# Retention scores without a repeated last chunk, weighed in four pieces instead of two

## The chip, the core and the metric

The kernel runs on one core of a Trainium2 chip. A core has a matrix engine (TensorE, PE in the profile), a vector engine (VectorE, DVE), an activation engine (ScalarE, ACT), a general engine (GpSimd, POOL) and a queue engine that issues the transfers (SyncE, SP). Each has its own list of instructions and runs it in order; they meet at semaphores. PE writes into PSUM, which has eight banks here, each 128 partitions by 512 float32 words. The metric is the device time of one execution in microseconds (us).

## The reference

Two blocks in a row, in float32. The first is retention with a decay per head, the second a gated feed-forward network on the result:

```
q, k, v: (8, 8, 576, 64)          batch, heads, positions, head size
scores = q @ k.T / sqrt(64)       per batch and head, 576 x 576
D[i, j] = gamma_head ** (i - j) if i >= j else 0
ret = scores * D
attn = ret @ v                    -> x of 4608 tokens x 512
xn = x / sqrt(mean(x * x) + 1e-6) * rms_g
out = (silu(xn @ w_gate) * (xn @ w_val)) @ w_out      512 -> 1536 -> 512
```

## The kernel before

**Retention in chunks.** The 576 positions of a head are cut into nine chunks of 64 (`NC` = 9, `L` = 64). Inside a chunk the kernel computes the 64x64 scores and weighs them (the decay and the causal triangle); what earlier chunks give to later ones goes through a 64x64 state per chunk, k transposed times v, that is carried on with a decay. Two heads make one job: with 8 batches and 4 pairs of heads there are 32 jobs, `j` = 0 to 31. `FIRST` is 8, so "the ninth job on" means `j` >= 8, 24 jobs.

**Where a product sits in the array.** Head `e` of the pair has its q and k in partitions `side(e)`, that is 0 to 63 or 64 to 127. All products of retention are 64x64, so each uses a quarter of the PE array: a half of its rows (where the operands lie) and a half of its columns (where the result goes in PSUM). A float32 product shows in the profile as two weight loads and two matmul records.

**The steps of a job:**

- `scores(j)` (product in line 295): for chunk `c` and head `e` the result goes to bank `s[e]`, partitions `side(c odd)`, columns 64 i on, with `i` = c // 2. Nine chunks leave the last column block (256 to 319) with its lower partitions alone, since there is no tenth chunk. The loop therefore runs to `NC + 1` = 10 and repeats chunk 8 for the upper partitions: 20 products for the two heads.
- `states(j)` (line 318): 16 products k.T v, into bank `s[2]`, into the free right part of `s[1]` and into bank `last`.
- `weigh(j)` (line 331): DVE multiplies the scores by a power of gamma and by the triangle and writes tile `ret`, 128 partitions by 5 x 64 for each head. One operation per head, 128x320. `ret` has one buffer.
- `sums(j)` (lines 362 and 344 for `j` >= 8): eight DVE operations that run along the chunks, each on the one before, and read the states out of PSUM.
- `values(j)` (line 382): 18 products of `ret` and v into two banks `av`. Odd chunks read partitions 64 to 127 of `ret`, even ones 0 to 63; for chunk 8, which is even, only partitions 0 to 63 of the last block are read, and v comes from the small tile `vt`.
- `carried(j)` (line 402): 16 products of `sum` and q that add onto `av`; ACT then copies `av` to x (line 426).

**The order.** `slot(j)` puts a job's work on the engines: values(j-1), scores(j), states(j), weigh(j), carried(j-1), sums(j). So a job's `ret` and `sum` are used one slot later. Jobs 0 to 11 are placed by a list of steps (`PLAN`) in the first 250 us, among the preparation of the weights and plain products (`up_plain`, line 762). The later jobs are placed by loops at the end: for each token block `u` from 2 on, six calls of `up(u, n)`, each with seven products of eight records (line 702, banks x, y, z, x, w, z, w), and a slot after some of them. After `up` comes `across` (line 872). DVE adds the products of `up` up (lines 709 and 721) and takes differences (line 786).

**Banks.** All PSUM tiles turn round one pool of eight banks. A slot takes six (two av, three s, one last), an `up` four (x, y, z, w). So the banks that `scores` fills are, one `up` later, the banks of the next products, and PE may write them only when DVE has read them. The framework finds these waits by itself from the regions that instructions read and write, and puts them on instructions; where one instruction has more waits than it can hold, a separate waiting instruction (EVENT_SEMAPHORE in the profile) is put in front.

Of the kernel before, what the change touches and what calls it, by code (L numbers as in the profile page):

```python
# [13 lines left out]
ALU = mybir.AluOpType  # L14
P = 128
L = P // 2
# [3 lines left out]
def _gamma(H):  # L20
    return 1.0 - 2.0 ** (-5.0 - np.arange(H, dtype=np.float64))
# [23 lines left out]
def kernel(  # L45
# [11 lines left out]
    nc = tc.nc  # L57
    B, H, S, D = q.shape
# [4 lines left out]
    NC = S // L  # L63
    NFULL = S // P
    TAIL = S - NFULL * P
# [7 lines left out]
    FIRST = 2 * NHP  # L73
# [15 lines left out]
    def bank(name):  # L89
        return banks.tile([P, 512], F32, tag="b", name=name)  # L90
# [23 lines left out]
    causal = const.tile([P, L], F32, name="causal")  # L114
# [167 lines left out]
    def side(i):  # L282
        return slice(i * L, i * L + L)
# [3 lines left out]
    def scores(j):  # L287

        d = st[j]
        s = d["s"] = [bank(f"s_{j}_{i}") for i in range(3)]  # L290
        for c in range(NC + 1):
            i, odd = divmod(c, 2)
            c = min(c, NC - 1)
            for e in range(2):
                nc.tensor.matmul(  # L295
                    s[e][side(odd), i * L : i * L + L], lhsT=d["kT"][side(e), c * L : c * L + L],
                    rhs=d["qT"][side(e), c * L : c * L + L], start=True, stop=True,
                )
# [24 lines left out]
    def weigh(j):  # L323

        d = st[j]
        hp = jobs[j][1]
        s = d["s"]
        n = NFULL + 1
        ret = d["ret"] = att.tile([P, 2, n, L], F32, tag="ret", name=f"ret_{j}", bufs=1)
        for e in range(2):  # L330
            nc.vector.scalar_tensor_tensor(
                out=ret[:, e], in0=s[e][:, : n * L].rearrange("p (c k) -> p c k", k=L),
                scalar=float(_gamma(H)[2 * hp + e] ** -L),
                in1=causal.unsqueeze(1).to_broadcast([P, n, L]), op0=ALU.mult, op1=ALU.mult,
            )

    def sums(j):

# [95 lines left out]
    def slot(j, rest=True):  # L434

        if rest:
            values(j - 1)
        scores(j)
        states(j)
        weigh(j)  # L440
        if j < FIRST:
            sums(j)
        if rest:
            carried(j - 1)
        if j >= FIRST:
            sums(j)
# [959 lines left out]
```

## Time and profile before

| | |
|---|---|
| time, median of 3 runs | 1101.61 us (1100.7 to 1102.21) |
| the profiled execution: its time, its span | 1100.22 us, 1098.4 us |
| granted TensorE clock, mean | 0.997 |
| ACT busy, POOL busy | 328.2 us (30%), 443.8 us (40%) |
| DMA, HBM | mean 222 GB/s; 211.92 MB read, 30.08 MB written |
| products of `up_plain`, line 762 | 384 records, 594 ns mean |
| products of `up`, line 702 | 2352 records, 379 to 382 ns mean by tile |

The page of a profile gives the busy time of each engine, its share of the span, the chain of work that ended last, and groups of instructions by line. The timeline lists instructions in order of time, with equal ones that follow each other merged: start, length, engine, line, operation, tiles, shape, count, and in brackets how long the engine had been idle before and what ended that. Matmuls overlap, so the merged length of a group is from its first start to its last end, and the distance from one start to the next says more than a length.

### The profile page before, as it was taken

The numbers are of one execution on the slowest core, as the hardware profiler recorded it, in microseconds if no ns is written. First come the engines' busy times: TensorE is split into PE (matmuls) and PEld (weight loads), VectorE is DVE, ScalarE is ACT, GpSimd is POOL, SyncE is SP. The second block draws the span as 40 slices with busy tenths as digits, with TensorE's granted clock in tenths as the row PEclk, the third lists the DMA queues.
The fourth block names the chain that finished last, engine by engine and source line by source line (L and its number), as shares of the span: only waits on it lengthen the run. The fifth ranks groups of instructions, "written<-read, shape, count | busy, mean of one in ns | idle before, by whom it ended". The sixth has DMA issues, their size and how long they took to land.

```text
span 1098.4 us, 24471 instructions
## 1 busy us (share of the span) xinstructions
PE 1085.5 (99%) x10102; PEld 912.2 (83%) x10102; DVE 727.2 (66%) x1251; ACT 328.2 (30%) x739; POOL 443.8 (40%) x421
## 2 busy tenths in 40 slices
PE   9899999999999999999999999999999999999998
PEld 7744444479988899889988998899888988998898
DVE  3878468877866774677667855677565735674467
ACT  5755564331124412332034203330233111201110
POOL 0026326538430195027702571237321932383236
PEclk9999999999999999999999999999999999999999
DMA  8756787596978876797678865888475755585471
GB/s 210 178 190 235 297 252 214 194 354 176 292 276 226 221 256 225 185 240 241 245 217 200 290 257 148 243 255 291 136 204 198 280 194 174 195 287 160 146 250 42
DMA packets 253871, 243.60 MB, mean 222 GB/s; under 512 B 193216, under 2 KB 213824, under 8 KB 247616
## 3 DMA queue, kind: packets, MB, share of 16 engines
q1 hardware_dynamic: 252320, 241.64, 69.7%
q8 instruction: 79, 1.29, 0.5%
q10 hardware_dynamic: 1440, 0.40, 0.2%
q14 instruction: 32, 0.26, 0.1%
HBM read 211.92 MB, written 30.08 MB: 220 GB/s over the span
## 4 chain that ended last, share of the span: by engine, by line
PE 97%; DVE 1%; issue 1%; ACT 0%; POOL 0%; POOLq 0%; DVEq 0%; ACTq 0%
PE up L762 15%; PE x L702 14%; PE w L702 13%; PE z L702 13%; PE y L702 7%; PE xo L872 6%; PE xp L872 4%; PE zo L872 4%; PE zp L872 3%; PE wo L872 2%; PE yo L872 2%; PE av L382 2%; PE av L402 2%; PE wp L872 2%; PE s L295 2%; PE yp L872 2%
## 5 line engine op out<-in xcount | busy, mean ns | idle before, releaser
L762 PE MATMUL up<-x,ring 128*128 128x512 f32 x384 | 167.1, 594 | 0.0
L702 PE MATMUL x<-x,ring 128*128 128x256 f32 x672 | 161.0, 382 | 0.0
L702 PE MATMUL w<-sums,ring 128*128 128x256 f32 x672 | 158.9, 379 | 0.0
L702 PE MATMUL z<-x,ring 128*128 128x256 f32 x672 | 158.7, 379 | 0.0
L824 POOL TENSOR_TENSOR vi<-h 128x384 f32<-128x384 f32 x32 | 42.4, 1326 | 275.9 <-DVE h L721 266.4
L762 PEld LDWEIGHTS up<-x,ring 128*128 128x128 f32 x384 | 72.2, 190 | 89.3 <-issue 84.7
L702 PEld LDWEIGHTS z<-x,ring 128*128 128x128 f32 x672 | 127.7, 190 | 17.4
L702 PEld LDWEIGHTS w<-sums,ring 128*128 128x128 f32 x672 | 127.6, 190 | 17.4
L702 PEld LDWEIGHTS x<-x,ring 128*128 128x128 f32 x672 | 125.3, 190 | 17.5 <-ACT m L728 0.2
L829 POOL TENSOR_TENSOR vi<-h 128x384 f32<-128x384 f32 (+2 forms) x46 | 43.9, 954 | 149.2 <-DVE h L721 149.2
L1068 POOL TENSOR_TENSOR vi<-vi 128x512 f32<-128x512 f32 (+1 forms) x77 | 78.2, 1028 | 51.9 <-DVE vi L899 35.5
L702 PE MATMUL y<-sums,ring 128*128 128x256 f32 x336 | 79.4, 379 | 0.0
L728 ACT COPY m<-x 128x512 f32<-128x512 f32 x42 | 24.6, 587 | 173.3 <-PE x L702 173.3
L709 DVE TENSOR_TENSOR h<-u,w 128x512 f32<-128x512 f32 x42 | 28.9, 688 | 67.8 <-PE w L702 67.8
L702 PEld LDWEIGHTS y<-sums,ring 128*128 128x128 f32 x336 | 63.8, 190 | 8.7
L709 DVE TENSOR_TENSOR u<-m,y 128x512 f32<-128x512 f32 x42 | 28.8, 686 | 63.2 <-PE y L702 62.5
L723 ACT ACTIVATE h<-h 128x512 f32<-128x512 f32 x63 | 39.7, 629 | 83.3 <-DVE h L709 83.3
L1188 POOL TENSOR_TENSOR vi<-vi 128x512 f32<-128x512 f32 (+1 forms) x24 | 40.7, 1696 | 30.4 <-DVE vi L1177 16.9
L709 DVE TENSOR_TENSOR u<-u,z 128x512 f32<-128x512 f32 x42 | 28.9, 687 | 33.6 <-PE z L702 33.4
L1188 POOL TENSOR_TENSOR ring<-ring 128x512 f32<-128x512 f32 x24 | 30.4, 1273 | 49.6 <-DMA w_up_blocks<-ring 43.9
L426 ACT COPY x<-av 128x192 f32<-128x192 f32 (+6 forms) x136 | 37.8, 278 | 30.0 <-PE av L402 28.5
L829 POOL TENSOR_TENSOR vi<-h,vi 128x384 f32<-128x384 f32 (+2 forms) x46 | 44.5, 968 | 3.6
(327 smaller groups left out, 2039.2 us busy)
## 6 DMA issues: line engine op xcount, KB each, us to landing
ring<-w_out_blocks SPq DMA_DIRECT2D x59, 1344.0 KB, 6.4
ring<-w_up_blocks SPq DMA_DIRECT2D x42, 1792.0 KB, 7.7
w_out_blocks<-vi SPq DMA_DIRECT2D x21, 448.0 KB, 6.2
out_dram<-vi SPq DMA_DIRECT2D x64, 128.0 KB, 3.1
qraw<-in_q_dram SPq DMA_DIRECT2D x96, 72.0 KB, 4.7
kraw<-in_k_dram SPq DMA_DIRECT2D x96, 72.0 KB, 2.7
k<-in_k_dram SPq DMA_DIRECT2D x48, 128.0 KB, 2.8
v<-in_v_dram SPq DMA_DIRECT2D x48, 128.0 KB, 3.1
```

Of the source, the lines that this page charges most:

```text
L295: nc.tensor.matmul(s[e][side(odd), i * L : i * L + L], lhsT=d["kT"][side(e), c * L : c * L + L], rhs=d["qT"][side(e), c * L : c * L + L], ...
L426: nc.scalar.copy(out=o, in_=part)
L702: nc.tensor.matmul(ps[:, i * HU : i * HU + HU], lhsT=w[:, PLACE[blk], c, i * P : i * P + P], rhs=t_of[u][blk][:, c], start=(start and i == ...
L709: nc.vector.tensor_tensor(out=o, in0=a, in1=pairs_of(ps), op=ALU.add)
L723: nc.scalar.activation(out=o, in_=c, func=AF.Silu)
L728: nc.scalar.copy(out=s1, in_=pairs_of(x_))
L762: nc.tensor.matmul(ps, lhsT=w[:, PLACE[blk], c % 2, i * P : i * P + P], rhs=x_of[u][:, c], start=(c == 0), stop=(c == NHP - 1),)
L824: eng.tensor_tensor(out=i1, in0=x12, in1=x11, op=ALU.subtract)
L829: eng.tensor_tensor(out=o[:, c], in0=a[:, c], in1=b[:, c], op=op)
L872: nc.tensor.matmul(ps, lhsT=lhs[:, c], rhs=w[:, s, c], start=((nm, s // 4) not in first), stop=False, skip_group_check=True,)
L1068: eng.tensor_tensor(out=t[:, :, o], in0=t[:, :, x], in1=t[:, :, y], op=ALU.add)
L1188: nc.gpsimd.tensor_tensor(out=t[o], in0=t[x], in1=t[y], op=op)
```

## The change

From the ninth job on, `scores` runs over the nine chunks alone: 18 products instead of 20. The upper partitions of the last block are then never written, so `weigh` may not read them: it weighs the four full blocks of each head in one operation (128 partitions by 256), and the last block in one more (64 partitions by 64). Jobs 0 to 7 keep the 20 products and the two operations.

```
-        for c in range(NC + 1):
+        for c in range(NC + (j < FIRST)):
...
-        for e in range(2):
-            nc.vector.scalar_tensor_tensor(
-                out=ret[:, e], in0=s[e][:, : n * L].rearrange("p (c k) -> p c k", k=L),
-                scalar=float(_gamma(H)[2 * hp + e] ** -L),
-                in1=causal.unsqueeze(1).to_broadcast([P, n, L]), op0=ALU.mult, op1=ALU.mult,
-            )
+        cuts = [(P, 0, n)] if j < FIRST else [(P, 0, NFULL), (TAIL, NFULL, n)]
+        for p, a, z in cuts:
+            for e in range(2):
+                nc.vector.scalar_tensor_tensor(
+                    out=ret[:p, e, a:z],
+                    in0=s[e][:p, a * L : z * L].rearrange("p (c k) -> p c k", k=L),
+                    scalar=float(_gamma(H)[2 * hp + e] ** -L),
+                    in1=causal[:p].unsqueeze(1).to_broadcast([p, z - a, L]),
+                    op0=ALU.mult, op1=ALU.mult,
+                )
```

Set side by side, the instruction lists of the two programs differ on two engines. On PE 48 products are gone, and there are 22 more separate waiting instructions: in the 20 calls of `up` that follow a slot, the first product into bank z now waits for DVE and for PE itself (an earlier product, some 40 products back), where before it waited for DVE alone; the other two stand in the part placed by the list. On DVE 48 operations 128x320 are replaced by 48 of 128x256 and 48 of 64x64. ACT, POOL and SP have the same instructions in the same order.

## The prediction

> **What bounds the kernel now.** I read the page first. PE is busy in 99% of the span, and the chain that ended last is PE.
>
> ```profile
> PE 1085.5 (99%) x10102; PEld 912.2 (83%) x10102; DVE 727.2 (66%) x1251; ACT 328.2 (30%) x739; POOL 443.8 (40%) x421
> ...
> PE 97%; DVE 1%; issue 1%; ACT 0%; POOL 0%; POOLq 0%; DVEq 0%; ACTq 0%
> ```
>
> So time can come only from work that PE no longer does, or go into a new wait of PE. A busy PE may still hide slack between records, so I read one slot in PE's timeline, job 21's (values of 20 first):
>
> ```profile
> 561.65 0.69 PE L382 MATMUL av<-ret,v 64*64 64x64 f32 x32
> 562.17 0.23 PE L382 MATMUL av<-ret,vt 64*64 64x64 f32 x2
> 562.19 0.27 PE L295 MATMUL s<-qT,kT 64*64 64x64 f32 x2
> 562.23 0.23 PE L382 MATMUL av<-ret,vt 64*64 64x64 f32 x2
> 562.28 0.70 PE L295 MATMUL s<-qT,kT 64*64 64x64 f32 x36
> 562.80 0.23 PE L318 MATMUL s<-v,k 64*64 64x64 f32 x1
> 562.81 0.22 PE L295 MATMUL s<-qT,kT 64*64 64x64 f32 x2
> ...
> 563.90 0.48 PE L702 MATMUL x<-x,ring 128*128 128x256 f32 x1
> ```
>
> From 562.28 to 562.80 lie 36 records of scores in 0.525 us. A record alone lasts 0.218, so several run at once: four at a time, one on each quarter of the array, is nine steps of 0.0583 us. A quarter does one record per step. The two products of the last value chunk (four records, `vt`) sit on two quarters only, and still the next full step of scores comes two steps later (562.17 to 562.28, 0.11 us): a half-filled pack costs what a full one does.
>
> Next, a slot with more waits in front of its states (job 22, keys and values arriving later):
>
> ```profile
> 576.18 0.69 PE L382 MATMUL av<-ret,v 64*64 64x64 f32 x32
> ...
> 576.81 0.75 PE L295 MATMUL s<-qT,kT 64*64 64x64 f32 x38
> 577.38 0.59 PE L318 MATMUL s<-v,k 64*64 64x64 f32 x26
> ...
> 578.46 0.48 PE L702 MATMUL x<-x,ring 128*128 128x256 f32 x1
> ```
>
> It takes 2.28 us to the next `up`, against 2.25: here the states start after the last score, not among them. Read in the same way, 13 slots have 2.28, six 2.25, and three more (jobs 9, 14, 30: 3.10, 3.64, 2.36). Job 14's holds a pause of PE of 1.06 us inside `carried`, with no releaser named.
>
> Then DVE behind the first of these slots:
>
> ```profile
> 564.42 0.88 DVE L331 SCALAR_TENSOR_TENSOR ret<-s,causal 128x320 f32<-128x320 f32 x2
> 565.22 0.21 DVE L362 COPY sum<-s 128x64 f32<-128x64 f32 x1
> 565.47 1.86 DVE L344 SCALAR_TENSOR_TENSOR sum<-sum,gc,s 128x64 f32<-128x64 f32 x6
> 567.44 0.28 DVE L344 SCALAR_TENSOR_TENSOR sum<-sum,gc,last 128x64 f32<-128x64 f32 x1
> 567.73 0.69 DVE L709 TENSOR_TENSOR u<-m,y 128x512 f32<-128x512 f32 x1
> 569.38 0.69 DVE L709 TENSOR_TENSOR u<-u,z 128x512 f32<-128x512 f32 x1 [0.97 <-PE z L702]
> ```
>
> DVE works through without a gap until 568.42, then waits 0.97 us for PE. And the one place where PE waits for this chain, jobs 8 and 9, where two slots are only one `up_plain` apart:
>
> ```profile
> 204.70 0.75 DVE L1177 SCALAR_TENSOR_TENSOR vi<-ring,exp 128x256 f32<-128x256 f32 x2
> 205.37 0.88 DVE L331 SCALAR_TENSOR_TENSOR ret<-s,causal 128x320 f32<-128x320 f32 x2
> 206.17 0.21 DVE L362 COPY sum<-s 128x64 f32<-128x64 f32 x1
> 206.42 1.86 DVE L344 SCALAR_TENSOR_TENSOR sum<-sum,gc,s 128x64 f32<-128x64 f32 x6
> 208.07 0.62 PE L318 MATMUL s<-v,k 64*64 64x64 f32 x26 [0.39 <-issue]
> ```
>
> The states of job 9 reuse a bank that the sums of job 8 read, and PE starts them 0.1 us after the fifth of the six sums ended.
>
> **The change, part by part.** *48 products fewer on PE.* Count the products of one slot by quarter, as rows half and columns half. Rows 0, columns 0: values 5 (even chunks, head 0), scores 5 (even chunks, head 0), states 4, carried 4: 18. Rows 0, columns 1: 5 + 5 + 4 + 4 = 18. Rows 1: 4 + 5 + 4 + 4 = 17 on each column half. Now the slot's time: 36 records at 0.0583 are 2.10 us, and 2.25 is this plus the fill and the drain before `up`. So the slot's time agrees with the need of its fullest quarter. The removed pair sits on columns 1, one product on each rows half. That leaves 18, 17, 17, 16: the fullest quarter is untouched, and its neighbour only idles for two steps, as in the `vt` pack. Gain by this count: 0. If PE went by the number of products in four-wide packs instead, a pack is gone, 2 x 0.0583 = 0.117 us, times 24 = 2.8 us. These are the ends; I take 0, because the `vt` pack is the nearest row and shows the half-filled price.
>
> *The gap before the states.* In the 13 slots of 2.28 us (and jobs 14 and 30, of the same kind) the states lose 0.036 us because PE has not passed their waits when the scores run out. With four records fewer to issue, PE's queue comes to these waits a step, 0.058, earlier, while the scores' fullest quarter ends when it did: the 0.036 should vanish, 14 x 0.036 = 0.5 us gained. Other end: the four records were cover, and the gap grows by their step, 24 x 0.058 = 1.4 us lost. I take -0.5, since the quarter that ends last does not move.
>
> *22 more waiting instructions on PE.* Queued behind each of the 20 in `up` are the z product and all of PE's later work. Its first term, PE itself, is some 40 products old; its second, DVE, is the weighing: ended at 565.30, needed by z at 567.46, so 2.16 us are left. 33 such instructions of line 702 exist already, each 51 ns on PE's queue, and products go on starting 1.72 or 1.73 us apart across them: PE's queue runs ahead of the array. Cost 0; the other end is in the rivals.
>
> *Weighing in four.* The trace has no 64x64 operation of this kind. Two 128x320 start 0.88 - 0.48 = 0.40 us apart, two 128x256 (line 1177) 0.75 - 0.417 = 0.333 apart. The 64 columns between them are 0.067, so the part that doesn't depend on size is 0.067 and 64 columns make 0.134. Four operations then take 2 x 0.333 + 2 x 0.134 = 0.93 instead of 0.80: +0.13 us per job. Upper end: the copy of 64 columns, after which the next started 0.25 us later: 2 x 0.333 + 2 x 0.25 = 1.17, +0.37. The new ones do not read each other as the copy's successor does, so I take +0.13: 3 us of DVE over 24 jobs.
>
> [...]
>
> What hides it: in `up`, the 0.97 us that DVE waits for z at 569.38. `u<-m,y` in front of it goes late by 0.13, and PE's next products still start in their step of 1.73 us up to the slot at 576.18, so none of them waits for it. `ret` is needed at 576.18, the sums at 577.86. If that cover were gone, 0.13 x 24 = 3 us would show. Cover is missing once, at job 8: its sums move by 0.13, the states of job 9 with them, and all PE work behind. +0.13 us (to +0.37).
>
> **Sum.** 0 - 0.5 + 0 + 0.13 = -0.4 us. The profiled execution took 1100.22 (span 1098.4 and 1.8 around it), so 1099.8. It is 1.4 below the median of the three runs; against that median, 1101.61, I forecast 1101.2.
>
> **Rivals.** *A. PE is limited by the count of packs.* Every job saves 0.117 us: 1101.6 - 2.8 = 1098.8. For it: nine steps of scores are exactly nine packs of four. Against it: the `vt` pack, the only half-filled one in the trace.
>
> *B. The waiting instruction in front of z stops PE (slower).* Place: the third product of `up`, after 20 slots. Price: in front of the states of job 22 PE's queue has two waiting instructions that start 0.125 us apart; if PE's queue has no lead there, 20 x 0.125 = 2.5 us, 1104.1. It decides only when the queue's lead is below that time, or the weighing more than 2.16 us late. Against it: eight records of 0.215 us lie before z, and the like instructions in front of x cost nothing.
>
> *C. The unexplained pause goes or comes again.* Job 14's slot took 3.64 - 2.28 = 1.36 us too long, with PE waiting for nothing that is shown; with 74 PE instructions fewer, whatever in the order of PE's list brings it may fall elsewhere. One pause less gives 1099.8, one more 1102.6. For it: one such slot among 22. Against a larger share: only one.
>
> That the change does not do what it says is excluded: the lists show 48 products fewer.
>
> **How the numbers follow.** Forecast 0.70, A 0.07, B 0.06, C gone 0.09, C again 0.08. About 0.2%, 2.2 us, is what a measurement of this kernel can tell from no change. Faster by more than that (below 1099.4) is A and a little of C with the forecast's gain: 0.08. Slower (above 1103.8) is B and two pauses: 0.07. Within: 0.85. The range takes in both cases of C with the unknown ends of the small terms (0.4): 1099.4 to 1103.0; A and B lie outside.
>
> **What would show it.** Slots of 2.25 us from 561 on, also where there were 2.28: right. Slots of 2.13: A is right and my count by quarters wrong. Slots of 2.28 or more where they were 2.28: the cover argument is wrong. The start of z more than 1.73 us after y: B. DVE's wait for z shrinking from 0.97 to about 0.84 shows the weighing's price; PE's gap at 208 growing from 0.39 to about 0.5 shows the one place where it counts. The prediction fails if PE stops anywhere else for over 0.1 us per job.

## The result, and the profile after

| | before | after |
|---|---|---|
| median of 22 runs each | 1101.62 us | 1099.76 us |
| ratio, with its 95% interval | | 0.998 (0.9972 to 0.9988) |
| the profiled execution: time, span | 1100.22, 1098.4 us | 1099.84, 1098.0 us |
| start of job 8's slot | 201.22 us | 202.61 us |
| from there to the end of the span | 897.22 us | 895.35 us |
| slot of job 9 | 3.101 us | 3.235 us |
| slot of job 14 | 3.643 us | 2.248 us |
| slot of job 30 | 2.358 us | 2.248 us |
| slots with the wait before the states (job 22) | 2.281 us | 2.248 us |
| slots without (job 21) | 2.245 us | 2.238 us |

The changed kernel is 1.9 us (0.2%) faster, where 0.4 was forecast. The interval of the ratio makes this 1.3 to 3.1 us. The time lies in the range, but the gain is over four times the forecast one, and the table says where. The forecast for the profiled execution, 1099.8, was met at 1099.84 by accident: before job 8 this execution is 1.39 us later than the one of before, and from job 8 on it is 1.87 us shorter. A second profile of each kernel (first experiment below) has the start of before 3 us elsewhere, but the second part within 0.2 us for both. So the second part is the one to read, and it agrees with the medians.

On the page of after, three lines matter: the busy times, the chain of work that ended last, and the queue that brings instructions (packets, MB, share of time):

```profile
PE 1085.8 (99%) x10006; PEld 911.3 (83%) x10006; DVE 729.9 (66%) x1299; ACT 328.2 (30%) x739; POOL 443.8 (40%) x421
...
PE 97%; DVE 1%; ACT 1%; issue 1%; POOL 0%; POOLq 0%; DVEq 0%; ACTq 0%
...
q8 instruction: 79, 1.29, 0.5%
```

PE lost 96 records and is still busy 99% of the span; DVE has 48 operations more and 2.7 us more of busy time. The totals say no more than that, since the two executions differ in their start.

The sums by stretch, before and then after, from job 8's slot to the end (length; PE, weight loads, DVE, ACT, POOL busy; clock; DMA share; GB/s):

```profile
201.22:1098.44 897.22, 891.16 (x8429) 806.77 (x8428) 588.31 (x976) 210.08 (x502) 381.77 (x364) 1.00 0.69 219
```

```profile
202.61:1097.96 895.35, 890.02 (x8333) 805.84 (x8332) 591.19 (x1024) 210.05 (x502) 381.76 (x364) 1.00 0.70 220
```

PE's idle time in this stretch was 897.22 - 891.16 = 6.06 us and is 5.33: a pause of 1.06 us less, and 0.35 us more at job 9 (both shown below). The other 1.14 us are time in which only some of PE's records ran, so they need the slots. The clock is the same and explains nothing.

PE's timeline in the slot of job 21, which had no gap before, and then that of job 22, which had one:

```profile
561.55 0.69 PE L386 MATMUL av<-ret,v 64*64 64x64 f32 x32
...
562.18 0.69 PE L295 MATMUL s<-qT,kT 64*64 64x64 f32 x33
562.66 0.28 PE L318 MATMUL s<-v,k 64*64 64x64 f32 x3
562.71 0.22 PE L295 MATMUL s<-qT,kT 64*64 64x64 f32 x1
...
563.79 1.99 PE L706 MATMUL x<-x,ring 128*128 128x256 f32 x8
...
576.07 0.69 PE L386 MATMUL av<-ret,v 64*64 64x64 f32 x32
...
576.70 0.75 PE L295 MATMUL s<-qT,kT 64*64 64x64 f32 x34
577.24 0.62 PE L318 MATMUL s<-v,k 64*64 64x64 f32 x26
...
578.32 0.92 PE L706 MATMUL x<-x,ring 128*128 128x256 f32 x3
```

Both now take 2.24 to 2.25 us to the next `up`. In job 21's slot two whole products of scores are gone and the time is the same to 0.007 us: the removed pair cost nothing. In job 22's slot 0.033 us went; that is the gap in front of the states.

The same place on DVE:

```profile
564.32 1.00 DVE L333 SCALAR_TENSOR_TENSOR ret<-s,causal 128x256 f32<-128x256 f32 x4
565.25 0.20 DVE L366 COPY sum<-s 128x64 f32<-128x64 f32 x1
565.49 1.86 DVE L348 SCALAR_TENSOR_TENSOR sum<-sum,gc,s 128x64 f32<-128x64 f32 x6
...
567.65 0.68 DVE L713 TENSOR_TENSOR u<-m,y 128x512 f32<-128x512 f32 x1
569.27 0.69 DVE L713 TENSOR_TENSOR u<-u,z 128x512 f32<-128x512 f32 x1 [0.94 <-PE z L706]
```

(The first row takes its shape from the first of four operations; two of them are 64x64.) From the start of the weighing to the copy is 0.93 us, before it was 0.80. The wait for z is still 0.94 us.

And job 14, in PE's timeline of before and then of after:

```profile
343.92 0.69 PE L382 MATMUL av<-ret,v 64*64 64x64 f32 x32
...
345.60 0.63 PE L402 MATMUL av<-qT,sum 64*64 64x64 f32 x26
347.29 0.34 PE L402 MATMUL av<-qT,sum 64*64 64x64 f32 x6 [1.06 <-issue]
347.56 0.70 PE L702 MATMUL x<-x,ring 128*128 128x256 f32 x2
```

```profile
345.38 0.69 PE L386 MATMUL av<-ret,v 64*64 64x64 f32 x32
...
347.03 0.67 PE L406 MATMUL av<-qT,sum 64*64 64x64 f32 x32
347.63 1.13 PE L706 MATMUL x<-x,ring 128*128 128x256 f32 x4
```

The pause of 1.06 us between the 26th and the 27th record of `carried` is gone, and with it 1.40 us of the slot: three quarters of all that the change brought. The account from job 8 on: job 9 +0.13, job 14 -1.40, job 30 -0.11, jobs 10 and 11 -0.04, the other slots -0.43 together; with -0.02 for job 8's slot and rounding, -1.87.

### The profile page after: what moved, and what is told of

The parts are those of the page before. It is cut to its first block, busy times and chain, and to the rows that moved or that the text cites. A ratio compares the mean times of both kernels' runs of the same rounds, so it can differ in the third digit from the quotient of the medians.

```text
span 1098.0 us, 24349 instructions
## 1 busy us (share of the span) xinstructions
PE 1085.8 (99%) x10006; PEld 911.3 (83%) x10006; DVE 729.9 (66%) x1299; ACT 328.2 (30%) x739; POOL 443.8 (40%) x421
## 4 chain that ended last, share of the span: by engine, by line
PE 97%; DVE 1%; ACT 1%; issue 1%; POOL 0%; POOLq 0%; DVEq 0%; ACTq 0%
PE up L766 15%; PE x L706 14%; PE w L706 13%; PE z L706 13%; PE y L706 7%; PE xo L876 6%; PE xp L876 4%; PE zo L876 4%; PE zp L876 3%; PE wo L876 2%; PE yo L876 2%; PE av L386 2%; PE wp L876 2%; PE av L406 2%; PE s L295 2%; PE yp L876 2%
## 5 line engine op out<-in xcount | busy, mean ns | idle before, releaser
L333 DVE SCALAR_TENSOR_TENSOR ret<-s,causal 128x256 f32<-128x256 f32 (+2 forms) x112 | 32.0, 336 | 22.3 <-PE s L295 22.3
```

Source lines behind the costliest of these rows:

```text
L333: nc.vector.scalar_tensor_tensor(out=ret[:p, e, a:z], in0=s[e][:p, a * L : z * L].rearrange("p (c k) -> p c k", k=L), scalar=float(_gamma( ...
```

## The experiments

**Both kernels again, unchanged.** If the pause is an accident of one execution, it moves or vanishes when the same kernel runs again; if it belongs to the program, it stays.

> The kernel before, unchanged, with a new profile. Theory P (the pause of job 14's slot belongs to the place: it is PE waiting for the next stretch of its own instruction list, and where such a stretch ends inside a slot is fixed by the list): the slot of job 14 takes 3.3 to 3.7 us again, the slots with two waits 2.28, job 9's 3.10. Theory R (the pause is an accident of one execution): job 14's slot takes 2.28, and a pause stands elsewhere or nowhere. Time ratio to the kernel before 1.000 in both.

> The changed kernel, unchanged, with a new profile. P: no slot after job 9's is over 2.3 us, job 9's 3.23; from job 8's slot to the end 895.4 us as in its first profile, 1.8 less than before; ratio 0.998. R: a pause of about 1 us in some slot as often as in the kernel before; ratio 0.9995 (the forecast's -0.5 us).

Before again: ratio 0.9999 (0.9988 to 1.001), rest from job 8 on 897.04 us. After again: 0.9979 (0.9968 to 0.999), rest 895.39. (Here and below a ratio is to executions of the kernel before that were measured along with that run.) PE's timeline of before, run again, in job 14:

```profile
348.68 0.63 PE L402 MATMUL av<-qT,sum 64*64 64x64 f32 x25
350.16 0.34 PE L402 MATMUL av<-qT,sum 64*64 64x64 f32 x6 [0.85 <-issue]
```

The job's slot starts 3.03 us later than in the first profile, and the pause stands in front of the same six records: it follows the program, not the clock on the wall. Counted from the start, 3394 of PE's matmul records stand in front of it both times ("at record 3394" from here on). Its length does change: 0.85 us instead of 1.06, and the slot takes 3.474 us instead of 3.643, so in this second pair job 14 is worth 1.23 us of 1.65. Job 30's slot takes 2.282 us here, like its kind; the 0.08 us above that were of the first execution alone. In after no pause over 0.18 us is found between 250 us and 1085 us, in either execution. So the 1.4 us are a property of the two lists of instructions.

**Tiny products at the start, to shift PE's list.** If the place in the list decides, more instructions at its head move the pause. `warm_up(n, 2)` adds n products of two columns at the very start; everything is still computed.

```
         warm_up(j == 0, 2 * P)
+        warm_up(12 * (j == 0), 2)
```

This is in the kernel of before; in that of after 11 and then 6 such products stand in the same place.

> The kernel before with 12 more tiny warm-up products (48 instructions) in job 0's turn, so that everything later stands 48 places further in PE's list; nothing else changes. P: the pause leaves job 14's slot (2.28 us) and may come in another; if it comes in none, the time from job 8's slot to the end is 1.4 us less and the ratio 0.9987 to 1.000. R: the shift does nothing; the pause comes or not as in the kernel before.

> The changed kernel with 11 more tiny warm-up products (44 instructions), which puts job 14's slot back to the place in PE's list that it has in the kernel before. P: job 14's slot takes 3.3 to 3.6 us, the others 2.25; 1.1 to 1.4 us slower than the changed kernel, ratio to the kernel before 0.9993. R: all slots 2.25, ratio as the changed kernel's.

> The changed kernel with 6 more tiny warm-up products (24 instructions), about half way back to the place that job 14's slot has in the kernel before. P (the place decides): job 14's slot takes a pause of 0 to 1.4 us, the same in every execution, and the time from job 8's slot to the end is 895.4 plus that pause; other slots 2.24 to 2.25. If the pause is of the same length as with 44 instructions (3.6 us slot), the place is a range of over 20 instructions; if there is none, it is narrower.

| | ratio to before (interval) | job 14 | pause found | from job 8 on |
|---|---|---|---|---|
| before + 12 | 1.0044 (1.0027 to 1.006) | 2.281 | job 22: slot 3.965; also 0.59 in `up`, and 0.40 in `across`, with ACT named as releaser | 899.19 |
| after + 11 | 1.0024 (1.0012 to 1.0035) | 3.627 | job 14; job 16: slot 2.470 | 897.04 |
| after + 6 | 1.0012 (1.0001 to 1.0023) | 2.248 | job 30: slot 3.573 | 896.73 |

PE's timeline of after with 11 tiny products, at job 14, and with 6, at job 30:

```profile
349.59 0.66 PE L407 MATMUL av<-qT,sum 64*64 64x64 f32 x30
351.31 0.32 PE L407 MATMUL av<-qT,sum 64*64 64x64 f32 x2 [1.06 <-issue]
```

```profile
809.88 0.66 PE L407 MATMUL av<-qT,sum 64*64 64x64 f32 x29
811.55 0.33 PE L407 MATMUL av<-qT,sum 64*64 64x64 f32 x3 [1.00 <-issue]
```

Eleven tiny products (22 records) bring the pause back into the changed kernel, at record 3392, two from where before had it. The stretch from job 8 on is back at 897.04, the same as before's in its second profile; of the 1.69 us that this is more than in after, job 14's slot makes 1.38 and job 16's 0.22. Without them record 3394 of after lies at 352.48 us, inside `up`, where nothing stops. With six, job 14 is free and job 30 pays. So the changed kernel's own work neither has nor lacks the pause; what decides is how its instructions fall along the list. That a slot other than job 14's would pay was not expected there. Twelve in the kernel of before took it out of job 14 and put a longer one into job 22:

```profile
582.59 0.67 PE L403 MATMUL av<-qT,sum 64*64 64x64 f32 x32
584.87 1.99 PE L703 MATMUL x<-x,ring 128*128 128x256 f32 x8 [1.61 <-DVE sum L345]
```

(The releaser named here can't be what it waited for: in job 21's slot of before the same product starts at 563.90, ahead of the sums, which begin at 565.47.) One thing speaks against "always record 3394": in this kernel that record also lies inside job 14's slot, at 351.67 us, and no pause is there. A fixed number of records is therefore not the rule; the last section counts all of PE's instructions, and finds a rule that fits all these pauses. All three kernels also start 2 to 3 us later (their excess by the medians less what is seen from job 8 on), which is not explained and which puts the ratio with 11 above the 0.9993 expected.

**Twenty products, weighed in four.** Undoes the first half of the change:

```
-        for c in range(NC + (j < FIRST)):
+        for c in range(NC + 1):
```

> Half of the change: weighed in four operations, but still 20 products. Theory Q (the gain per slot comes from the scores' end: the last pack is half filled, so PE's queue reaches the waits before the states earlier): slots stay 2.28 and 2.25 as in the kernel before, job 9's grows by the weighing's 0.13 to 3.23. Rival W (the waits that the new regions bring change the slots): slots change without a product being removed.

Ratio 0.9995 (0.9985 to 1.0005); job 9 3.228 us, slots 2.281 and 2.245 as before, rest 897.47. PE's timeline at job 14:

```profile
346.96 0.55 PE L406 MATMUL av<-qT,sum 64*64 64x64 f32 x24
348.85 0.34 PE L406 MATMUL av<-qT,sum 64*64 64x64 f32 x8 [1.34 <-issue]
```

The four weighings alone cost 0.13 us at job 9 and nothing elsewhere; the gaps before the states are those of 20 products, and the pause is in job 14 as with them, here 1.34 us long (slot 3.853). It is two records earlier, at 3392. Four more separate waiting instructions stand ahead of it in this list than in that of before, and two records are four instructions of the list (each has a weight load), so as many instructions stand ahead of it as before. At 3392 it is also in the two other kernels with the added waiting instructions that have it in job 14, the one above with 11 tiny products and the one below with the pair on the other columns.

**Twenty products, the repeated pair first.** Is the gap of 0.036 us due to the half-filled pair at the end of the scores, right in front of the states, or to four records more that PE has to issue before it reaches the waits? Here the pair is made first; the count stays, two operations weigh:

```
-        for c in range(NC + (j < FIRST)):
+        order = list(range(NC + 1))
+        if j >= FIRST:
+            order = [NC] + order[:NC]
+        for c in order:
...
-        cuts = [(P, 0, n)] if j < FIRST else [(P, 0, NFULL), (TAIL, NFULL, n)]
+        cuts = [(P, 0, n)]
```

> 20 products and two operations as in the kernel before, but the repeated pair of products comes first in the scores instead of last. Q: the scores end with a half-filled pack, so slots with two waits take 2.25 as in the changed kernel, although no product is gone. Rival N (the gain is that of two products fewer to issue): 2.28 as in the kernel before.

Ratio 0.9999 (0.9988 to 1.001). PE's timeline of it at job 22:

```profile
578.02 0.69 PE L389 MATMUL av<-ret,v 64*64 64x64 f32 x32
...
578.65 0.75 PE L298 MATMUL s<-qT,kT 64*64 64x64 f32 x38
579.23 0.58 PE L321 MATMUL s<-v,k 64*64 64x64 f32 x26
...
580.31 0.92 PE L709 MATMUL x<-x,ring 128*128 128x256 f32 x3
```

The slot takes 2.29 us, so the half-filled pair at the end is not what makes the gap. The number of records in front of the waits is the explanation that is left; with the pair left out the gap is gone. The pause is at 3394, in job 14, again.

**Twenty products, the repeated pair on the other columns.** The forecast rests on the count by quarter of the array. Here the last chunk's pair is made twice on columns 0, so the fullest quarter has 19 products instead of 18, with the same number of products as before; four operations weigh:

```
-        for c in range(NC + (j < FIRST)):
-            i, odd = divmod(c, 2)
+        for c in range(NC + 1):
+            i, odd = divmod(c if j < FIRST else min(c, NC - 1), 2)
```

> The changed kernel with the last chunk's pair of products made twice into the same place, columns 0, so that 20 products load the quarters 19, 17, 18, 16. Count by quarters: every slot 0.117 us longer than the changed kernel's 2.25, that is 2.36; 24 x 0.117 = 2.8 us slower than it. Count by packs of four: 20 products are five packs, 2.28 as in the kernel before.

Ratio 1.0019 (1.0005 to 1.0033). PE's timeline at job 22:

```profile
575.84 0.69 PE L386 MATMUL av<-ret,v 64*64 64x64 f32 x32
...
576.47 0.81 PE L295 MATMUL s<-qT,kT 64*64 64x64 f32 x37
577.06 0.28 PE L318 MATMUL s<-v,k 64*64 64x64 f32 x3
...
578.19 1.13 PE L706 MATMUL x<-x,ring 128*128 128x256 f32 x4
```

2.355 us in every slot of both kinds but three (job 9's 3.128, job 14's with the pause 3.636, job 19's 2.667); that is 0.107 more than job 22's slot takes with the pair left out. The same two products cost 0.007 us where quarters idle (job 21's kind) and 0.107 to 0.117 on the fullest quarter (2.355 against 2.248 and 2.238).

**Eighteen products in all jobs.** The change extended to jobs 0 to 7:

```
-        for c in range(NC + (j < FIRST)):
+        for c in range(NC):
...
-        cuts = [(P, 0, n)] if j < FIRST else [(P, 0, NFULL), (TAIL, NFULL, n)]
+        cuts = [(P, 0, NFULL), (TAIL, NFULL, n)]
```

> The changed kernel with 18 products and four weighing operations in jobs 0 to 7 too. If what is left of the gain is PE's records alone: jobs 0 to 7 gain up to 8 x 0.03 = 0.3 us, ratio to the kernel before 0.9977. If DVE or the place in PE's list decides there (8 x 7 = 56 instructions fewer ahead of job 8): the first 200 us move by more than 0.3 us either way, and a slot after job 8's may take a pause of 1 to 1.5 us again.

1099.9 us, ratio 0.9983 (0.997 to 0.9996): no better than the changed kernel's 0.998. No slot has a pause, but job 8's slot takes 1.70 us instead of 1.20, job 9's 3.44, and the calls of `up` behind jobs 14 and 27 lose 0.39 and 0.34 us. From job 8 on it takes 896.91 us, 1.56 more than after; what lies before is 2.27 us shorter. No version that was run beats after. Eighteen products with two weighings wasn't tried, because the second half of the last block would be read unwritten, nor a layout with 17 products on the fullest quarter, because two quarters on different rows would then write one region of a bank, and products on different quarters can start out of the list's order (by 0.05 us in job 21's slot, shown in the last section).

## Why the prediction was right or wrong

**The step that went wrong is the pause, rival C.** The prediction took "the unexplained pause" as something that "goes or comes again" by chance, priced it at 1.36 us, and gave its vanishing 0.09 because it was "one such slot among 22". The price was about right: 1.40 measured, and 1.23 in the second pair of profiles. The judgement was wrong. One slot among 22 in one execution says how rare the pause is along the list, not whether the same program has it each time. It has it each time (two profiles of before, and three lists of 20 products without the tiny ones). It is gone in the changed kernel each time (two profiles), and shifting the list by 22 records brings it back. So the sum lacked a term of -1.4, and -0.4 became -1.9 by the medians. The measured 1099.76 is what the prediction gave for C gone, 1099.8; the time lies in the range because the range took this case in, not because the sum had it. The text did name the cause's likely carrier, "the order of PE's list"; a forecast that followed that thought would have given C a much larger share, though nothing that it had read told the sign. By the rule of the last section, found only from all the runs, the sign can be counted from the two lists.

**The products, 0: right, and shown.** The slots without gap moved by 0.007 us. The last experiment but one put the pair on the fullest quarter and found the 0.117 step that the forecast had by quarters. Rival A, packs of four, falls: it wanted slots of 2.13 us in after, and no change at all when the pair goes to the other columns. The row that the prediction leaned on was read too simply: two records of scores start at 562.19 beside those of `vt`, so that pack was more than half-filled. It is the experiment that shows the count by quarters, not that row.

**The gap before the states, -0.5: right.** 0.033 us per slot instead of 0.036, 0.46 over the 14 slots. (All slots but jobs 9 and 14 gave 0.60, with 0.08 at job 30 that the second pair doesn't have.) The reason given, four records fewer ahead of the waits, fits the kernel with the pair first, which rules out the pair's place; the waits themselves were not moved in any run. The other end, cover lost, did not occur.

**22 more waiting instructions, 0: right.** In job 21's `up` the products in z start at 567.35, 1.73 us after those in y at 565.62, as before. Rival B falls.

**The weighing, +0.13: right in both places.** 0.93 us from its start to the copy, as worked out. Job 9's slot grew by 0.134, and by 0.127 with 20 products and four weighings. The operations of 64x64 last 0.20 us each, and the next thing starts 0.13 us after each (job 21 in after: 564.98, 565.12, the copy at 565.25), so they overlap. They don't read each other, which may be why; that was argued and not tried.

**Two signs that were announced didn't show as written, though their step held.** DVE's wait for z was to shrink from 0.97 to 0.84, and is 0.94. `u<-m,y`, the operation in front of that wait, started 0.29 us after the last of the sums before and 0.20 after it now: by this working there were 0.09 us in which DVE waited for y (its products end at 567.62 by before's timeline), too short to be listed as a wait; the prediction had DVE without a gap there. They took up most of the 0.13, so `u<-m,y` is late by 0.03 against PE's work (3.86 us after the first product in x, before 3.83), which is what the wait for z lost. And PE's gap in front of job 9's states was to grow from 0.39 to 0.5, and is 0.74. DVE's and PE's timelines of after there:

```profile
206.76 1.00 DVE L333 SCALAR_TENSOR_TENSOR ret<-s,causal 128x256 f32<-128x256 f32 x4
207.69 0.21 DVE L366 COPY sum<-s 128x64 f32<-128x64 f32 x1
207.94 1.86 DVE L348 SCALAR_TENSOR_TENSOR sum<-sum,gc,s 128x64 f32<-128x64 f32 x6
```

```profile
207.44 0.76 PE L386 MATMUL av<-ret,v 64*64 64x64 f32 x29
...
208.15 0.69 PE L295 MATMUL s<-qT,kT 64*64 64x64 f32 x33
209.58 0.62 PE L318 MATMUL s<-v,k 64*64 64x64 f32 x26 [0.74 <-issue]
```

The states start 209.58 - 207.44 = 2.14 us after the values, before 208.07 - 206.06 = 2.01: the 0.13 of the sums. The rest of the longer gap is work that ended earlier: the scores begin 0.71 us after the values instead of 0.83, which isn't explained, and last 0.69 instead of 0.79. A gap grows at both of its ends; only the later one is on the path.

## What to carry to other kernels

Count small products by the quarter of the array they use: here the fullest quarter set the time, and two products on the others were worth 0.007 us, where on the fullest they cost 0.107 to 0.117. A pause of the main engine with no releaser named is no noise until the same program has been profiled twice; if it stays, a change of the instruction list can win or lose it (here eleven tiny products at the list's head put 1.38 us back into job 14's slot), and a gain of its size says nothing about the edit. Look at the packets of the instruction queue around it (here PE went on 1.26 to 1.58 us after one had landed). Compare two executions from a common point behind the start, since the start alone moved by 3 us here.

## What the runs showed of the hardware

**A pause that belongs to the instruction list.** PE stops for 0.59 to 1.6 us with its data ready, at a place that a program keeps and that a few more instructions at its head move. Where and when it stops, over all the traces, shows what it stops for: the next piece of its own list. The traces keep the time of every packet. The queue of instructions (q8 on the page) brings packets of 16 KB: 79 in before, 80 in before with 12 tiny products, 78 in the kernel with eighteen products in all jobs. PE's lists there have 20376, 20425 and 20153 instructions (weight loads, products and waiting instructions), which is 255 to 258 for a packet. 256 fits all three, and it fits the places: each of the nine pauses has a number of PE's instructions in front of it that is 192 or 193 more than a multiple of 256. Such a place is called a step here. PE goes on 1.26 to 1.58 us after a packet has landed; what fills this time is not seen.

| pause | instructions of PE in front | packet on its way, us | PE goes on, us |
|---|---|---|---|
| before, job 14 | 6848 | 345.03 to 345.95 | 347.29 |
| before again, job 14 | 6848 | 347.71 to 348.65 | 350.16 |
| before + 12, job 22 | 11713 | 582.34 to 583.40 | 584.87 |
| before + 12, `up` | 14529 | 715.50 to 716.48 | 717.90 |
| after + 11, job 14 | 6849 | 348.91 to 349.87 | 351.31 |
| after + 6, job 30 | 16321 | 808.71 to 809.97 | 811.55 |

The three kernels of 20 products without tiny ones have their pauses at 6848 too. Counted in order, there are as many packets as steps, and the n-th packet belongs to step n + 1. From 250 us on no step in any of the eleven traces is passed sooner than 1.26 us after the landing of its packet. A packet starts about when PE passes the step before (within 4.2 us of it from 250 us on in before and after, by the median 0.8 and 0.2 us after it; 1.0 in job 14 of before), so PE catches up with its packets where it runs 256 instructions fastest: a slot has 273 to 283 of them in some 2.3 us, an `up` 112 in 12 us. Among the slots of jobs 10, 11 and 13 to 31 in all eleven traces, 17 hold two steps (one at the very end counted); eight of these have a pause over 0.8 us, and the 214 others have none. In after no slot holds two, and none has a pause; the same is true of the kernel with eighteen products in all jobs. In before with 12 tiny products job 14's slot holds one step, so record 3394 lies there without a pause. Why the other nine slots with two steps pay little or nothing is not settled; in job 29 of before the packet was on its way at 791.36, before the slot began at 792.56, while in job 14 it started 1.11 us after the slot.

**Order on PE.** In job 21's slot of after, three records of the states start at 562.66 and the last record of the scores at 562.71. So products on different quarters don't start strictly in the order of the list. DVE's 1251 operations in before all start in the order of its list, by their lines.

**The start.** The point where job 8's slot begins differs by 3 us between two profiles of the same kernel of before, and by 0.01 between the two of after. Six to twelve products of two columns at its head put it, by the medians, 2 to 3 us later. What sets it stays open.
